# Four chunks of an attention and two-MLP kernel: values placed right behind scores

## The chip, the cores and the metric

One core of a Trainium2 chip runs the whole program. The metric is the device time of one execution in microseconds; lower is better. Matmuls run on TensorE (PE; PEld is its weight load), and the other engines are VectorE (DVE), ScalarE (ACT), GpSimd (POOL) and SyncE (SP), whose queue issues most DMAs.

## The reference, cut to what matters

```python
scores = einsum('bhij,hg->bgij', scale * q @ k.T, w_pre)      # 2 batches, 12 heads, 448 rows, 64 wide
attn = exp(scores - max(scores)); attn = attn / sum(attn)
attn = einsum('bhij,hg->bgij', attn, w_post)
x = (attn @ v) laid out as [896, 768]
h = x @ w_in;  y = (h * clip(h + 3, 0, 6) / 6) @ w_out          # MLP 1, 2048 wide
h = y @ w2_in; out = (P(h) / Q(h)) @ w2_out                     # MLP 2, a rational activation
```

Heads are mixed before and after the softmax (w_pre, w_post), so the twelve heads of a row are needed together.

## The kernel before, in words

The query rows are cut into eight chunks: chunks 0 to 3 of batch 0 and 4 to 7 of batch 1. Six of them have 120 rows, and chunks 3 and 7 have 88. A chunk is worked off in groups of ten rows, twelve groups in a long chunk and nine in a short one. Ten rows times twelve heads fill 120 partitions, and one group is one step of the loop `for s in range(G)`.

In a step for group m, TensorE does the head mix before the softmax, "premix" (lines 306 to 308: three products of one 448-column bank, from the split halves `sh` and `sl` that GpSimd made three groups ahead, lines 294 and 296). VectorE takes the row maximum (line 310), ScalarE the exponential with its sum (line 312). VectorE turns the sum into a reciprocal (lines 320 and 321, `norm`), and ScalarE scales the second mixing matrix with it (line 325, `weigh`, the tile `wr`). Two steps later (`LAG`) TensorE uses it in the "postmix" (line 341: four products, eight instructions, into a bank with the tag A). At the top of the step after that the bank is emptied into `at` by ScalarE (line 348) or, in groups listed in `BYV`, by VectorE (line 346).

Between these steps lie visits of other work. A visit of scores is two calls of `scores` for the next chunk (line 271: twelve products of 64 rows, for four heads). Its banks (tag sc) are copied to `stg` by ScalarE and VectorE in turn (line 274) and spread by DMA into `full`, the layout by row groups (line 252). A visit of values is two calls of `av_unit` for the chunk before (line 363: 32 products with 64 columns, four heads). Its sums `X` are split into a rounded part by ScalarE (line 379) and a remainder by VectorE (line 380). Each `av_unit` also issues on SP the load of values four head pairs ahead (`load_v`, line 136).

In a chunk of twelve steps the scores come in steps 1, 3 and 5 (`SST`) and the values in steps 7, 9 and 11 (`AVST`). So a step with a visit, called heavy here, is always followed by a light one. The queries of the chunk after next are split in steps 9 to 11 (`q_prep` put down for steps 8 and 9; lines 244 on ScalarE and 245 on VectorE). At the end of chunk 2 the keys of batch 1 are split too (lines 236 and 237). From the end of chunk 6 on, pieces of the MLP weights are converted (lines 435 to 460), and ScalarE copies finished rows (line 513).

Every engine works in the order in which the code issues its instructions (`manual_schedule`). `posts`, `xposts`, `aposts`, `preps` and `lows` are lists of work that a step hands to the next one. `full_step` says whether the next step issues `norm` and `weigh` of the group before at its top, ahead of its own maximum, or behind it.

```python
LAG = 2
ONES, BYV = [1, 3, 5], (5, 7, 9)
SST = {12: [1, 1, 3, 3, 5, 5], 9: [0, 0, 2, 2, 4, 4]}
QST = {12: [8, 9], 9: [6, 7]}
AVST = {12: [7, 7, 9, 9, 11, 11], 9: [5, 5, 7, 7, 8, 8]}
AVLAST = [2, 2, 4, 4, 6, 6]
```

Of the kernel before, what the change touches and what calls it, by code (L numbers as in the profile page):

```python
# [7 lines left out]
F32 = mybir.dt.float32  # L8
# [11 lines left out]
B, H, S, D = 2, 12, 448, 64  # L20
JP, JC = 112, 4
GR = 10
GP = GR * H
CH = 120
NCH = 4
MG = CH // GR
NP = H // 2
# [21 lines left out]
def fused_kernel(  # L49
# [23 lines left out]
    chunks, parts = plan()  # L73
# [44 lines left out]
    vraw = {}  # L118
# [211 lines left out]
    def postmix(m):  # L330
# [13 lines left out]
        o = at[C][:, :, :, c0 : c0 + rr]  # L344
        if m in BYV:
            aposts.append(lambda: nc.vector.tensor_copy(out=o, in_=av))
        else:
            aposts.append(lambda: nc.scalar.activation(out=o, in_=av, func=AF.Copy))  # L348

    xps = {}  # L350

    def av_unit(C, h):
        b, r0, n, G = chunks[C]
        if h % 2 == 0:
            return
        if h % 4 == 1:
            tag = "sc" if C + 1 < len(chunks) or h == 1 else "A"
            xps[C] = ps.tile([128, 512], F32, tag=tag, bufs=BUFS[tag], name=f"X{C}_{h}")
        X = xps[C][:, : 2 * CH].rearrange("p (h n) -> p h n", n=CH)
        for jc in range(JC):  # L360
            for hh in (h - 1, h):
                vs = vraw[(C, hh // 2)][:, hh % 2, :].rearrange("p (c d) -> p c d", d=D)
                nc.tensor.matmul(  # L363
                    X[hh % 2 * D : hh % 2 * D + D, hh % 4 // 2, :n], lhsT=vs[:, jc, :], rhs=at[C][:, jc, hh, :n],
                    start=(jc == 0), stop=(jc == JC - 1),
                )
        load_v(*((C, h // 2 + 4) if h // 2 + 4 < NP else (C + 1, h // 2 + 4 - NP)))
        if h % 4 == 3:
            av_evac(C, h, X)

    def av_evac(C, h, X):
        b, r0, n, G = chunks[C]
        c0 = (h - 3) // 2
        t0 = b * S + r0
        src = X[:, :, :n]
        cs, ts_ = slice(c0, c0 + 2), slice(t0, t0 + n)
        o = (x1 if t0 < XRAW else XH)[:, cs, ts_]
        xposts.append([
            lambda: nc.scalar.activation(out=o, in_=src, func=AF.Copy),
            lambda: nc.vector.tensor_tensor(out=XL[:, cs, ts_], in0=src, in1=o.bitcast(F32), op=ALU.subtract),  # L380
        ])
# [190 lines left out]
    LAG = 2  # L572
    ONES, BYV = [1, 3, 5], (5, 7, 9)


    SST = {12: [1, 1, 3, 3, 5, 5], 9: [0, 0, 2, 2, 4, 4]}
    QST = {12: [8, 9], 9: [6, 7]}
    AVST = {12: [7, 7, 9, 9, 11, 11], 9: [5, 5, 7, 7, 8, 8]}
    VAT = 11
    AVLAST = [2, 2, 4, 4, 6, 6]  # L580
# [4 lines left out]
    m = 0  # L585
    for C, (b, r0, n, G) in enumerate(chunks):
# [3 lines left out]
        def add(units, steps):  # L590
            for i, u in enumerate(units):
                sched.setdefault(steps[i * len(steps) // len(units)], []).append(u)

        sst = SST[G] if C else ONES
        if nxt is not None:
# [9 lines left out]
        if C > 0:  # L605
            add([lambda h=h: av_unit(C - 1, h) for h in range(1, H, 2)], [("av", a) for a in (AVST[G] if nxt is not None else AVLAST)])

        for s in range(G):
# [11 lines left out]
            if full_step:  # L620
                norm(m - 1)
                weigh(m - 1)
            for p in posts[:1] + xposts:
                p[0]()
            gsplit(m + 3)()
            if C:
# [13 lines left out]
            for p in posts[1:]:  # L640
                p[1]()
            full_step = bool(s in sst if nxt is not None else s >= 7) or ("av", s) in sched
            for p in xposts + lows:
# [10 lines left out]
            if m >= LAG:  # L654
                postmix(m - LAG)
            for u in sched.get(("av", s), []):
                u()
            for u in sched.get(s, []):
                u()
# [42 lines left out]
    pieces(2)  # L702
    for h in range(1, H, 2):
        av_unit(C, h)
        flush()
# [293 lines left out]
```

## Time and profile before

| what | value |
|---|---|
| median of three runs | 700.87 us (699.5 to 701.43) |
| the profiled execution, its own time | 697.88 us |
| its span, first to last instruction | 696.1 us |
| PE busy | 686.3 us (99%) |
| DVE busy | 532.7 us (77%) |
| ACT busy | 433.8 us (62%) |
| POOL busy | 168.2 us (24%) |
| granted clock of TensorE, mean | 1.000 |

The attention part takes the first 232 us of the span, and the two MLPs the rest. A line of the timeline begins with the start in us from the beginning of the span and the duration; in square brackets stands how long the engine was idle before it and what ended that. A "busy" PE is not one at its peak, because matmuls overlap in a pipeline; what a stage costs is read from the start of one group of products to the start of the next.

### The profile page before, as it was taken

The numbers are of one execution on the slowest core, as the hardware profiler recorded it, in microseconds if no ns is written. First come the engines' busy times: TensorE is split into PE (matmuls) and PEld (weight loads), VectorE is DVE, ScalarE is ACT, GpSimd is POOL, SyncE is SP. The second block draws the span as 40 slices with busy tenths as digits, with TensorE's granted clock in tenths as the row PEclk, the third lists the DMA queues.
The fourth block names the chain that finished last, engine by engine and source line by source line (L and its number), as shares of the span: only waits on it lengthen the run. The fifth ranks groups of instructions, "written<-read, shape, count | busy, mean of one in ns | idle before, by whom it ended". The sixth has DMA issues, their size and how long they took to land.

```text
span 696.1 us, 12343 instructions
## 1 busy us (share of the span) xinstructions
PE 686.3 (99%) x4460; PEld 616.2 (89%) x4461; DVE 532.7 (77%) x964; ACT 433.8 (62%) x881; POOL 168.2 (24%) x195
## 2 busy tenths in 40 slices
PE   8999999999999999999999999999999999999998
PEld 4779888888889888989889888898999999999997
DVE  6855685666657699999976556549999899989991
ACT  6767787787887455555543222237766667669851
POOL 2987775877776200000000000000000000000000
PEclk9999999999999999999999999999999999999999
DMA  5646486545394377675743332517666574755522
GB/s 200 232 133 175 138 215 197 163 139 165 120 265 124 113 246 213 199 218 183 230 156 121 121 122 88 184 54 273 212 240 211 180 267 166 243 181 207 190 81 90
DMA packets 76032, 122.81 MB, mean 176 GB/s; under 512 B 6804, under 2 KB 56260, under 8 KB 75972
## 3 DMA queue, kind: packets, MB, share of 16 engines
q1 hardware_dynamic: 75684, 121.66, 54.2%
q8 instruction: 35, 0.57, 0.3%
q10 hardware_dynamic: 288, 0.37, 0.1%
q14 instruction: 25, 0.20, 0.1%
HBM read 83.39 MB, written 19.27 MB: 147 GB/s over the span
## 4 chain that ended last, share of the span: by engine, by line
PE 93%; DMA 2%; DVE 2%; issue 1%; ACT 1%; POOL 0%; SPq 0%; POOLq 0%; DVEq 0%
PE h L389 11%; PE h L388 11%; PE h L387 11%; PE A L341 9%; PE acc L387 6%; PE acc L389 6%; PE acc L388 6%; PE y L388 6%; PE y L387 6%; PE y L389 6%; PE X L363 5%; PE sc L271 4%; PE M L306 3%; PE M L308 2%; PE M L307 2%; DMA vraw<-in_v_dram 1%
## 5 line engine op out<-in xcount | busy, mean ns | idle before, releaser
L389 PE MATMUL h<-xh,wl 128*128 128x512 f32 (+1 forms) x384 | 139.7, 364 | 0.0
L388 PE MATMUL h<-xl,wh 128*128 128x512 f32 (+1 forms) x384 | 139.5, 363 | 0.0
L387 PE MATMUL h<-xh,wh 128*128 128x512 f32 (+1 forms) x384 | 139.5, 363 | 0.0
L296 POOL TENSOR_TENSOR sl<-full,sh 120x448 fp32r<-120x448 f32 x87 | 100.0, 1149 | 7.3
L341 PEld LDWEIGHTS A<-wr,e 120*112 120x112 f32 x720 | 86.4, 176 | 8.0 <-ACT wr L325 4.0
L310 DVE TENSOR_REDUCE st<-M 120x1 f32<-120x448 f32 x90 | 56.0, 622 | 48.2 <-PE M L308 48.1
L341 PE MATMUL A<-wr,e 120*112 120x120 f32 x720 | 88.9, 266 | 2.2 <-ACT wr L325 2.2
L312 ACT ACTIVATE e<-M,st 120x448 f32<-120x448 f32 x90 | 57.1, 635 | 40.5 <-DVE st L310 34.4
L462 ACT ACTIVATE wh<-wf 128x768 fp32r<-128x768 f32 (+1 forms) x52 | 42.6, 819 | 62.0 <-PE y L388 46.6
L387 PEld LDWEIGHTS h<-xh,wh 128*128 128x128 f32 x384 | 72.1, 188 | 7.5
L388 PEld LDWEIGHTS h<-xl,wh 128*128 128x128 f32 x384 | 72.1, 188 | 7.6
L389 PEld LDWEIGHTS h<-xh,wl 128*128 128x128 f32 x384 | 72.1, 188 | 7.6
L435 ACT ACTIVATE wf<-wraw 128x768 f32<-128x768 f32 (+1 forms) x56 | 49.5, 883 | 42.9 <-DVE wl L463 40.8
L463 DVE TENSOR_TENSOR wl<-wf,wh 128x768 fp32r<-128x768 f32 (+1 forms) x52 | 49.6, 954 | 32.4 <-ACT wh L462 32.4
L388 PE MATMUL y<-gl,wh 128*128 128x384 f32 x192 | 70.1, 365 | 0.0
L387 PE MATMUL y<-gh,wh 128*128 128x384 f32 x192 | 69.9, 364 | 0.0
L389 PE MATMUL y<-gh,wl 128*128 128x384 f32 x192 | 69.5, 362 | 0.0
L294 POOL TENSOR_SCALAR sh<-full 120x448 fp32r<-120x448 f32 x87 | 54.0, 620 | 43.5 <-PE M L307 20.6
L443 DVE SCALAR_TENSOR_TENSOR wf<-wraw,icst,wf 128x768 int32<-128x768 int32 (+1 forms) x56 | 56.5, 1011 | 0.7
L439 DVE SCALAR_TENSOR_TENSOR wf<-wraw,icst,wf 128x768 int32<-128x768 int32 (+1 forms) x56 | 55.9, 999 | 0.9
L348 ACT ACTIVATE at<-A 112x480 f32<-112x480 f32 x87 | 50.3, 579 | 1.8 <-PE A L341 1.8
L389 PE MATMUL acc<-ws,xl 128*128 128x384 f32 x128 | 42.8, 334 | 0.0
(115 smaller groups left out, 1416.3 us busy)
## 6 DMA issues: line engine op xcount, KB each, us to landing
wraw<-in_moe_w_out_dram SPq DMA_DIRECT2D x28, 768.0 KB
wraw<-in_moe_w_in_dram SPq DMA_DIRECT2D x22, 768.0 KB
full<-stg SPq DMA_DIRECT2D x60, 210.0 KB
vraw<-in_v_dram SPq DMA_DIRECT2D x42, 224.0 KB
wpre<-in_moe_w_in_dram SPq DMA_DIRECT2D x10, 768.0 KB
w2h<-wh SPq DMA_DIRECT2D x16, 384.0 KB
w2l<-wl SPq DMA_DIRECT2D x16, 384.0 KB
ws<-w2h SPq DMA_DIRECT2D x16, 384.0 KB
```

Of the source, the lines that this page charges most:

```text
L294: eng.tensor_scalar(out=sh[:r], in0=s[:r], scalar1=1.0, scalar2=0.0, op0=ALU.mult, op1=ALU.add)
L296: return lambda: eng.tensor_tensor(out=sl[:r], in0=s[:r], in1=sh[:r].bitcast(F32), op=ALU.subtract)
L310: nc.vector.tensor_reduce(out=st[:r, 0:1], in_=mt[:r, :S], op=ALU.max, axis=AX.X, negate=True)
L312: nc.scalar.activation(out=e[:r], in_=mt[:r, :S], func=AF.Exp, bias=st[:r, 0:1], accum_out=st[:r, 1:2])
L341: nc.tensor.matmul(av[:, jc], lhsT=e[:r, jc * JP : (jc + 1) * JP], rhs=wr[:r, :, :rr], start=True, stop=True)
L348: aposts.append(lambda: nc.scalar.activation(out=o, in_=av, func=AF.Copy))
L387: nc.tensor.matmul(o, lhsT=wh, rhs=mh, start=first, stop=False)
L388: nc.tensor.matmul(o, lhsT=wh, rhs=ml, start=False, stop=False)
L389: nc.tensor.matmul(o, lhsT=wl, rhs=mh, start=False, stop=last)
L439: nc.vector.scalar_tensor_tensor(out=wi, in0=hw, scalar=icst[:, 0:1], in1=wi, op0=ALU.bitwise_and, op1=ALU.bitwise_or)
L443: nc.vector.scalar_tensor_tensor(out=wi, in0=lw, scalar=icst[:, 1:2], in1=wi, op0=ALU.logical_shift_right, op1=ALU.bitwise_or)
L463: nc.vector.tensor_tensor(out=lv, in0=w, in1=hv.bitcast(F32), op=ALU.subtract)
```

## The change

For chunks 2, 4, 5 and 6 (`joint`: long, not the first two and not the last) the visits are placed anew. Scores come in steps 1, 3 and 6, values in steps 3, 6 and 9. In steps 3 and 6 the values stand right behind the scores, since the scores of a step are now issued before its values. The sums of the values go into a bank with the tag A (that of the postmixes) in these chunks, and into one with the tag sc in the others. In every step of such a chunk `norm` and `weigh` of the group before come at the top. Behind them, ahead of the step's own maximum, come all copies of the scores and both halves of the split of `X`. The postmixes of groups 2, 5, 8 and 9 of these chunks are emptied by VectorE, in steps 5, 8, 11 and step 0 of the next chunk. `av_unit` counts head pairs instead of heads, which changes no instruction.

```diff
--- before.py
+++ after.py
@@ -342,38 +342,35 @@
                 av[:, jc], lhsT=e[:r, jc * JP : (jc + 1) * JP], rhs=wr[:r, :, :rr], start=True, stop=True
             )
         o = at[C][:, :, :, c0 : c0 + rr]
-        if m in BYV:
+        if g in BYV.get(C, ()):
             aposts.append(lambda: nc.vector.tensor_copy(out=o, in_=av))
         else:
             aposts.append(lambda: nc.scalar.activation(out=o, in_=av, func=AF.Copy))
 
     xps = {}
 
-    def av_unit(C, h):
+    def av_unit(C, hp, wide, tag):
         b, r0, n, G = chunks[C]
-        if h % 2 == 0:
-            return
-        if h % 4 == 1:
-            tag = "sc" if C + 1 < len(chunks) or h == 1 else "A"
-            xps[C] = ps.tile([128, 512], F32, tag=tag, bufs=BUFS[tag], name=f"X{C}_{h}")
-        X = xps[C][:, : 2 * CH].rearrange("p (h n) -> p h n", n=CH)
+        i = hp % wide
+        if i == 0:
+            xps[C] = ps.tile([128, 512], F32, tag=tag, bufs=BUFS[tag], name=f"X{C}_{hp}")
+        X = xps[C][:, : wide * CH].rearrange("p (h n) -> p h n", n=CH)
+        vs = vraw[(C, hp)].rearrange("p h (c d) -> p h c d", d=D)
         for jc in range(JC):
-            for hh in (h - 1, h):
-                vs = vraw[(C, hh // 2)][:, hh % 2, :].rearrange("p (c d) -> p c d", d=D)
+            for k in range(2):
                 nc.tensor.matmul(
-                    X[hh % 2 * D : hh % 2 * D + D, hh % 4 // 2, :n], lhsT=vs[:, jc, :], rhs=at[C][:, jc, hh, :n],
+                    X[k * D : k * D + D, i, :n], lhsT=vs[:, k, jc, :], rhs=at[C][:, jc, 2 * hp + k, :n],
                     start=(jc == 0), stop=(jc == JC - 1),
                 )
-        load_v(*((C, h // 2 + 4) if h // 2 + 4 < NP else (C + 1, h // 2 + 4 - NP)))
-        if h % 4 == 3:
-            av_evac(C, h, X)
-
-    def av_evac(C, h, X):
+        load_v(*((C, hp + 4) if hp + 4 < NP else (C + 1, hp + 4 - NP)))
+        if i == wide - 1:
+            av_evac(C, hp - i, hp + 1, X)
+
+    def av_evac(C, p0, p1, X):
         b, r0, n, G = chunks[C]
-        c0 = (h - 3) // 2
         t0 = b * S + r0
         src = X[:, :, :n]
-        cs, ts_ = slice(c0, c0 + 2), slice(t0, t0 + n)
+        cs, ts_ = slice(p0, p1), slice(t0, t0 + n)
         o = (x1 if t0 < XRAW else XH)[:, cs, ts_]
         xposts.append([
             lambda: nc.scalar.activation(out=o, in_=src, func=AF.Copy),
@@ -570,12 +567,14 @@
             aposts.pop(0)()
 
     LAG = 2
-    ONES, BYV = [1, 3, 5], (5, 7, 9)
+    ONES = [1, 3, 5]
+    BYV = {0: (5, 7, 9), **{C: (2, 5, 8, 9) for C in (2, 4, 5, 6)}}
 
 
     SST = {12: [1, 1, 3, 3, 5, 5], 9: [0, 0, 2, 2, 4, 4]}
     QST = {12: [8, 9], 9: [6, 7]}
     AVST = {12: [7, 7, 9, 9, 11, 11], 9: [5, 5, 7, 7, 8, 8]}
+    SSTJ, AVSTJ = [1, 1, 3, 3, 6, 6], [3, 3, 6, 6, 9, 9]
     VAT = 11
     AVLAST = [2, 2, 4, 4, 6, 6]
     full_step = False
@@ -591,7 +590,8 @@
             for i, u in enumerate(units):
                 sched.setdefault(steps[i * len(steps) // len(units)], []).append(u)
 
-        sst = SST[G] if C else ONES
+        joint = C > 1 and nxt is not None and G * GR == CH
+        sst = SSTJ if joint else SST[G] if C else ONES
         if nxt is not None:
             kw = {} if C else {"first": nc.vector.tensor_copy}
             add([lambda h=h: scores(nxt, h, **kw) for h in range(0 if C else FIRST, NP)], sst)
@@ -603,7 +603,9 @@
         if C == NCH - 1:
             add([lambda h=h: k_prep(1, h) for h in range(4, NP)], [0, 1])
         if C > 0:
-            add([lambda h=h: av_unit(C - 1, h) for h in range(1, H, 2)], [("av", a) for a in (AVST[G] if nxt is not None else AVLAST)])
+            tag = "A" if joint else "sc"
+            avst = AVSTJ if joint else AVST[G] if nxt is not None else AVLAST
+            add([lambda h=h: av_unit(C - 1, h, 2, tag) for h in range(NP)], [("av", a) for a in avst])
 
         for s in range(G):
             if s == (5 if C == 1 else 0) and C and C + 2 < len(chunks):
@@ -620,8 +622,14 @@
             if full_step:
                 norm(m - 1)
                 weigh(m - 1)
-            for p in posts[:1] + xposts:
+            first = posts if joint else posts[:1]
+            for p in first + xposts:
                 p[0]()
+            if joint:
+                for p in first + xposts:
+                    p[1]()
+                posts.clear()
+                xposts.clear()
             gsplit(m + 3)()
             if C:
                 for p in posts[:1]:
@@ -639,7 +647,7 @@
                 p[0]()
             for p in posts[1:]:
                 p[1]()
-            full_step = bool(s in sst if nxt is not None else s >= 7) or ("av", s) in sched
+            full_step = joint or bool(s in sst if nxt is not None else s >= 7) or ("av", s) in sched
             for p in xposts + lows:
                 p[1]()
             for p in preps:
@@ -653,9 +661,9 @@
                 next(wpieces)
             if m >= LAG:
                 postmix(m - LAG)
+            for u in sched.get(s, []):
+                u()
             for u in sched.get(("av", s), []):
-                u()
-            for u in sched.get(s, []):
                 u()
             if C == PRE and s == LATE - 1:
                 flush()
@@ -700,8 +708,8 @@
     drain()
     load_units(3)
     pieces(2)
-    for h in range(1, H, 2):
-        av_unit(C, h)
+    for h in range(NP):
+        av_unit(C, h, 2, "sc" if h < 2 else "A")
         flush()
     run(h110)
     h101 = ps.tile([128, 512], F32, tag="M", name="h1_0_1")
```

## Rows read from the trace of the kernel before

**Rows 1.** Page, part 1: busy us, share of the span, instructions.

```profile
PE 686.3 (99%) x4460; PEld 616.2 (89%) x4461; DVE 532.7 (77%) x964; ACT 433.8 (62%) x881; POOL 168.2 (24%) x195
```

**Rows 2.** Windows, chunks 2 and 5: us, busy by engine, clock, DMA share, GB/s.

```profile
67.10:94.93 27.83, 27.83 (x266) 24.21 (x265) 16.75 (x45) 21.84 (x60) 21.88 (x26) 1.00 0.63 176
...
145.92:173.81 27.89, 27.89 (x267) 24.70 (x265) 17.09 (x48) 21.28 (x60) 22.18 (x26) 1.00 0.52 154
```

**Rows 3.** Timeline of PE, chunk 5, steps 7 to 9 in part.

```profile
164.84 0.98 PE L341 MATMUL A<-wr,e 120*112 120x120 f32 x8
165.59 0.44 PE L306 MATMUL M<-sh,wp_h 120*120 120x448 f32 x1
...
166.27 0.98 PE L341 MATMUL A<-wr,e 120*112 120x120 f32 x8
167.18 1.86 PE L363 MATMUL X<-at,vraw 112*64 112x120 f32 x32
168.97 0.46 PE L306 MATMUL M<-sh,wp_h 120*120 120x448 f32 x1
```

**Rows 4.** Timeline, VectorE and ScalarE, one group from maximum to weights.

```profile
222.71 0.62 DVE L310 TENSOR_REDUCE st<-M 120x1 f32<-120x448 f32 x1 [1.00 <-PE M L308]
...
223.37 0.64 ACT L312 ACTIVATE e<-M,st 120x448 f32<-120x448 f32 x1 [0.51 <-DVE st L310]
...
224.13 0.15 DVE L320 TENSOR_SCALAR st<-st 120x1 f32<-120x1 f32 x1 [0.32 <-ACT e L312]
...
224.57 0.40 ACT L325 ACTIVATE wr<-wq,st 120x120 f32<-120x120 f32 x1
```

**Rows 5.** Timeline of VectorE, chunk 5: maximum of step 9, then remainders.

```profile
169.88 0.62 DVE L310 TENSOR_REDUCE st<-M 120x1 f32<-120x448 f32 x1 [1.58 <-PE M L308]
170.43 0.40 DVE L380 TENSOR_TENSOR xl<-X,x 128x240 fp32r<-128x240 f32 x1
170.74 1.42 DVE L245 TENSOR_TENSOR ql<-qraw,qr 128x270 fp32r<-128x270 f32 x1
```

**Rows 6.** Timeline of VectorE, chunk 0, where GpSimd stood idle.

```profile
34.75 0.52 DVE L245 TENSOR_TENSOR ql<-qraw,qr 128x360 fp32r<-128x360 f32 x1
```

**Rows 7.** Line 245 in chunks 4 and 5: count, ns min/median/max.

```profile
L245 DVE TENSOR_TENSOR ql<-qraw,qr x4: 833/1278/1418, 143.2 to 172.9; 128x360 fp32r<-128x360 f32 x2, 128x270 fp32r<-128x270 f32 x2
```

**Rows 8.** Timeline of GpSimd, the same stretch.

```profile
170.71 1.15 POOL L296 TENSOR_TENSOR sl<-full,sh 120x448 fp32r<-120x448 f32 x1
```

**Rows 9.** Line 346, postmix emptied by VectorE: count, ns min/median/max.

```profile
L346 DVE COPY at<-A x3: 656/656/658, 29.8 to 36.8; 112x480 f32<-112x480 f32 x3
```

**Rows 10.** Timeline of PE, chunk 0: four light steps in a row.

```profile
28.14 0.44 PE L306 MATMUL M<-sh,wp_h 120*120 120x448 f32 x1
...
30.80 1.07 PE L341 MATMUL A<-wr,e 120*112 120x120 f32 x8 [0.38 <-ACT wr L325]
...
35.14 0.44 PE L306 MATMUL M<-sh,wp_h 120*120 120x448 f32 x1
```

**Rows 11.** Timeline, end of chunk 2 and start of chunk 3.

```profile
90.08 0.47 PE L306 MATMUL M<-sh,wp_h 120*120 120x448 f32 x1
...
97.05 1.45 DVE L237 TENSOR_TENSOR xh<-kraw,xh 128x448 fp32r<-128x448 f32 x2
...
98.01 0.18 PEld L271 LDWEIGHTS sc<-xh,qr 64*120 64x120 f32 x2 [0.48 <-DVE xh L237]
98.41 0.46 PE L306 MATMUL M<-sh,wp_h 120*120 120x448 f32 x1
```

**Rows 12.** Timeline of PE, chunk 7, step 2.

```profile
206.27 1.07 PE L341 MATMUL A<-wr,e 120*112 120x120 f32 x8 [0.94 <-ACT wr L325]
```

**Rows 13.** Page, part 5: postmix emptied by ScalarE.

```profile
L348 ACT ACTIVATE at<-A 112x480 f32<-112x480 f32 x87 | 50.3, 579 | 1.8 <-PE A L341 1.8
```

**Rows 14.** Timeline of SP's queue, chunk 5: the last spreads.

```profile
162.03 1.61 SPq L252 DMA_DIRECT2D full<-stg  x2
```

**Rows 15.** Timeline of GpSimd, chunk 5, step 9: first split of chunk 6.

```profile
168.31 0.56 POOL L294 TENSOR_SCALAR sh<-full 120x448 fp32r<-120x448 f32 x1 [1.62 <-DMA vraw<-in_v_dram]
```

## The prediction

> **What bounds the kernel now.** I read the shares of busy time first: TensorE is busy for 99% of the span [rows 1]. Then the windows chunk by chunk: chunks 2 and 5 take 27.83 and 27.89 us and TensorE is busy in all of it, at full clock [rows 2]. Last the timeline. From one postmix to the next premix pass 0.75 us (164.84 to 165.59), from that premix to its postmix 0.68, so a light step costs 1.43 us of TensorE. A postmix with values behind it takes 0.91 (166.27 to 167.18), and the values 1.79 to the next premix [rows 3]. So TensorE is nowhere late in these chunks: light and heavy steps alternate, and each heavy one lets the others catch up. The change has no wait to remove there. All it can win is the entry into a visit, and it must not make TensorE wait.
>
> **Fewer visits.** The products stay the same in number and size. Behind a postmix the values start 0.91 - 0.75 = 0.16 us later than a premix would [rows 3]. Each of four chunks gives up two such entries, eight in all. From scores straight to values does not occur in the trace. If it costs as much as an entry, the gain is nothing; if it costs nothing and saves what leaving the scores costs as well (taken as a second 0.16), the gain is 8 x 0.32 = 2.6 us. I take one entry each: -1.3 us. The Trainium skill ("TensorEngine Tiling (Array Packing)", Key Properties) says that a change of tiling mode drains TensorE. Scores use 64 rows and values 64 columns, so by that rule the junction is a drain too and the gain stays at 8 x 0.16 or below, not at 2.6; the 0.16 above agrees that a change of mode costs something.
>
> **What it does to the order.** Heavy steps were 1, 3, 5, 7, 9 and 11; now they are 1, 3, 6 and 9. Light steps now stand in runs: 4 and 5, 7 and 8, and 10, 11 and 0, with step 1's own postmix behind them. In a run a step has 1.43 us. The chain of a group is longer: from the maximum to the exponential 0.66 us, from there to the reciprocal 0.76, from there to the weights 0.44 and 0.40 for them, 0.84 in all [rows 4]. With weights first the reciprocal stands at the head of VectorE's queue and waits for the exponential; the next maximum is queued behind it. That loop is 0.66 + 0.76 + 0.3 (the two small operations, part of the 0.44) = 1.7 us per step, 0.3 more than TensorE needs. Steps 4, 5, 7 and 8 come in pairs behind two visits, and the chain starts ahead of these; so I take 0 for them, at most one step's 0.3 for each of the eight pairs, 2.4.
>
> **The end of chunks 4 and 5.** Here the split of queries falls into steps 10 and 11, which were light and heavy and are now both light. Count from the premix of step 10. Its maximum starts 0.91 later (168.97 to 169.88) and VectorE is free 0.55 after that, at 1.45 [rows 3, 5]. Then comes a query remainder. It takes 0.52 while GpSimd is idle [rows 6], and 0.83 to 1.42 in these two chunks [rows 7], where a split of GpSimd runs beside it (170.71 to 171.86, with the remainder ending at 172.16) [rows 5, 8]. With 1.2 it ends at 2.65. Next is the postmix of group 8, new on VectorE, at 0.66 [rows 9]: 3.31. Only then comes the reciprocal of group 10, and its weights are there 0.84 later, at 4.15. TensorE wanted them at 2 x 1.43 + 0.68 = 3.54, so it waits 0.6. Then 0.3, the maximum of step 11 (0.55), a second remainder (1.2) and the postmix of group 9 (0.66) bring VectorE to 6.02 and the weights of group 11 to 6.86, wanted at 4.97 + 0.6 = 5.57: 1.3 more. Together 1.9 us. With remainders of 0.52 the same sum gives 0.5, with 1.42 it gives 2.3. Chunk 0 has four light steps in a row, with postmixes on VectorE: 28.14 to 35.14 is 7.00 us in place of 5.72, or 1.3 lost, and the wait is for the weights [rows 10]. I take that 1.3 for each chunk, 2.6 for both. The Trainium skill ("SBUF — State Buffer", Who interferes with whom) has VectorE and GpSimd share a port pair, and an operation of VectorE with two inputs there blocks against a reading GpSimd. The remainder that ended 0.30 after GpSimd's split fits that; since GpSimd splits nearly without pause in a light run, the rule would favour 1.9 over 1.3, 1.2 us more for both chunks.
>
> **The end of chunk 2.** From the premix of step 10 to that of chunk 3's step 1 are 8.33 us, and the scores wait for a key remainder on VectorE [rows 11]. In that time lies a values visit of 0.16 + 1.79 = 1.95 that now goes to an earlier place, where TensorE is the bound. If the rest stayed as it is, 6.4 would be left. VectorE's queue, though, holds up to the second key remainder three maxima (1.65), two query remainders (2.4), two postmixes (1.3), two reciprocals (0.6) and two key remainders (1.45 for a pair): 7.4, from 0.91 on, so to 8.3. The second scores follow and the premix 0.4 after (98.01 to 98.41). So 8.7 in place of 6.4: +2.3. With query remainders of 0.52 it is +0.9, with 1.42 +2.7.
>
> **The end of chunk 6.** Weight pieces and row copies load ScalarE and VectorE there, and TensorE already waits 0.94 for weights in step 2 of chunk 7 [rows 12]. A visit of 1.95 that covered this goes; two postmixes go from ScalarE to VectorE and give it 2 x 0.58 back [rows 13]: +0.8. At the least 0, at the most 1.95.
>
> **Queues.** The two loads of values now stand on SP ahead of the four spreads of that visit, and wait until the values are multiplied. The last two spreads take 1.61 us to issue and end at 163.64 [rows 14]; GpSimd's first split of the next chunk started 4.67 later, at 168.31 [rows 15]. Now four spreads (3.2) follow the values of step 6, and perhaps the two loads at up to 0.8 each; with the 4.67 that is 7.9 to 9.5 after the values. The split needs 1.7 more (0.56 and 1.15) [rows 8, 15], so 9.6 to 11.2. Step 0's premix wants its low half 2 x 1.43 + 3.4 + 2 x 1.43 + 0.45 (two of its products) = 9.6 after them. So it comes 0 to 1.6 late, in the stretch that VectorE already holds back by 0.6. I add nothing, up to 1.0 for each of four chunks. Loads of values come sooner than needed, which costs nothing. The bank of the sums is wanted two postmixes later, and its copies come at the top of the next step: 0.
>
> **Sum.** -1.3 + 0 + 2.6 + 2.3 + 0.8 = +4.4 us. The profiled execution took 697.88, its span and 1.8 around it that the change leaves alone; so 702.3. It was 3.0 under the median of the three runs; against 700.87 the forecast is 705.3 us. All low ends give -2.6 + 0 + 1.0 + 0.9 + 0 = -0.7, so 700.2; all high ends 0 + 2.4 + 4.6 + 2.7 + 2.0 + 4.0 = +15.7.
>
> **Rivals.**
> Faster: the ends cost nothing, since VectorE meets GpSimd idle and the weights of groups 10 and 11 arrive in time; the junction saves both costs. For it speaks that late spreads leave GpSimd idle just when the first remainder runs, which then takes 0.52. Against it, the second remainder still finds GpSimd splitting, and chunk 0 lost 1.3 in such a run. Place: the postmixes of groups 10 and 11; it decides when their weights come within 3.54 and 4.97 us of step 10's premix. Price: -2.6, so 698.3.
> No change: the ends cost their low values (0.5, 0.5, 0.9 and 0) and the entries give 1.3 back: +0.6, so 701.5.
> Spreads: the first split of the next chunk comes late, and each later one takes 1.7 against steps of 1.43. At the middle of the bound that is 0.5 in each of four places beyond what VectorE costs: +6.4, so 707.3. For it speaks that GpSimd waited 1.62 there already [rows 15]; against it, that this wait cost TensorE nothing.
>
> **How the numbers follow.** My forecast 0.44, the spreads 0.13, no change 0.25, faster 0.18. A measurement of this kernel tells about 0.3%, 2.1 us, from nothing. Slower by more than that are the first two: 0.57. Within it is the third: 0.25; faster the fourth: 0.18. For 8 times in 10 the range reaches from 698.9, just above the faster rival, to 708.3, the spreads with a little of the high ends. If the forecast's mechanism is the right one, 703 to 708.
>
> **What would show it.** Right: in chunks 4 and 5 no wait of TensorE until step 10, then two, at the postmixes of groups 10 and 11, for weights on ScalarE with VectorE's postmix or query remainder just ahead of the reciprocal; chunk 5 about 1 us above its 27.89; scores to values starting about 0.16 late. Wrong: no waits at chunk ends (then faster or no change), waits for GpSimd's halves in step 0 (the spreads), or waits in steps 4, 5, 7 and 8, where I put nothing.

## The result and the profile after

The changed kernel took 703.99 us (median of 7 runs, 703.65 to 707.75) against 700.43 (7 runs, 697.55 to 701.43) on the same chip: ratio 1.0063, 95% interval 1.0044 to 1.0082. It is slower, by 3.6 us between the medians and by 4.4 by the ratio. The forecast was 705.3, with 0.57 for slower. The profiled execution of the changed kernel has a span of 702.3, 6.2 more than before.

Part 1 of the page after, to set beside [rows 1]: busy us, share of the span, instructions.

```profile
PE 687.2 (98%) x4461; PEld 614.9 (88%) x4461; DVE 539.7 (77%) x980; ACT 433.6 (62%) x865; POOL 169.2 (24%) x195
```

TensorE's busy time hardly grew (686.3 to 687.2), so over 5 of the 6.2 are waits. Six rows of the view of waits, whose columns are us in total, times and longest. Before:

```profile
DVE st L310 <- PE M L308: 48.1, 66, 2.0
...
DVE st L320 <- ACT e L312: 19.4, 34, 0.8
...
PEld A L341 <- ACT wr L325: 4.0, 5, 1.3
...
PEld M L308 <- POOL sl L296: 1.4, 2, 0.9
...
PEld sc L271 <- DVE xh L237: 0.7, 2, 0.5
...
DVE xl L380 <- ACT x L379: 0.5, 2, 0.3
```

After:

```profile
DVE st L320 <- ACT e L312: 32.2, 46, 0.8
...
DVE st L310 <- PE M L308: 18.1, 23, 2.6
...
DVE xl L377 <- ACT x L376: 13.8, 14, 1.5
...
PEld A L341 <- ACT wr L325: 5.7, 8, 1.5
...
PEld M L308 <- POOL sl L296: 3.9, 6, 0.9
...
PEld sc L271 <- DVE xh L237: 3.2, 3, 2.2
```

The rows of VectorE have to be read together. Its maximum waited 48.1 us for TensorE's premix before and 18.1 after; but its reciprocal now waits 32.2 for ScalarE's exponential (19.4 before), and its half of the split of `X` 13.8 for ScalarE's (0.5 before). The three add up to 68.0 before and 64.1 after, and VectorE's idle time is 163.4 us of the span before and 162.6 after. So the fall of the first row shows the new order of VectorE's work, and it is no measure of what was lost. The rows of PEld are TensorE's own waits: for weights (ScalarE, behind VectorE's reciprocal), for GpSimd's low halves and for VectorE's key remainders. All three grew.

To place the time I listed the starts of all 90 premixes in both traces and took the differences. "C5 step 0" is from that premix to the next.

| place | before | after | change | forecast |
|---|---|---|---|---|
| a step of scores and one of values, against a merged and a light step (chunks 2, 5) | 6.37 and 6.39 | 6.20 and 6.22 | -0.17, eight times -1.4 | -1.3 |
| light steps 4, 5, 7, 8 | 1.45 | 1.42 to 1.46 | 0 | 0 |
| C2 step 10 to C3 step 1, less the visit of 1.95 | 6.38 | 9.05 | +2.7 | +2.3 |
| C3 step 3 | 1.45 | 1.85 | +0.4 | 0 |
| C4 step 10 to C5 step 2, less the visit of 1.5 | 7.35 | 9.17 | +1.8 | +1.3 |
| C5 step 10 to C6 step 2, less the visit | 7.33 | 7.67 | +0.3 | +1.3 |
| C6 step 10 to C7 step 3, less the visit | 10.38 | 11.29 | +0.9 | +0.8 |
| sum | | | +4.7 | +4.4 |

From chunk 2's first premix to the end of the span are 628.98 us before and 633.74 after, +4.76, so the table holds nearly all of it. The other 1.4 lie ahead of chunk 2, where both kernels issue the same work: 0.8 ahead of the first premix and 0.6 at the end of chunk 0 (more on that below).

**The merge.** Timeline of TensorE, chunk 5, the end of step 1 (scores alone) and step 3 (scores, then values):

```profile
154.56 0.46 PE L271 MATMUL sc<-xh,qr 64*120 64x448 f32 x2
...
155.96 0.46 PE L306 MATMUL M<-sh,wp_h 120*120 120x448 f32 x1
...
159.01 0.47 PE L271 MATMUL sc<-xh,qr 64*120 64x448 f32 x2
...
160.42 1.86 PE L361 MATMUL X<-at,vraw 112*64 112x120 f32 x32
162.21 0.46 PE L306 MATMUL M<-sh,wp_h 120*120 120x448 f32 x1
```

Scores to premix are 1.40, scores to values 1.41. The junction costs what leaving the scores costs anyway, so one entry is saved and not two.

**The end of chunk 2.** Timeline of VectorE and TensorE in part, with one of GpSimd's splits:

```profile
93.14 0.46 PE L306 MATMUL M<-sh,wp_h 120*120 120x448 f32 x1
...
94.78 0.91 DVE L245 TENSOR_TENSOR ql<-qraw,qr 128x360 fp32r<-128x360 f32 x1
...
96.95 0.66 DVE L245 TENSOR_TENSOR ql<-qraw,qr 128x360 fp32r<-128x360 f32 x1
...
97.31 1.30 POOL L296 TENSOR_TENSOR sl<-full,sh 120x448 fp32r<-120x448 f32 x1
...
97.53 1.56 DVE L237 TENSOR_TENSOR xh<-kraw,xh 128x448 fp32r<-128x448 f32 x1
...
99.02 0.53 DVE L183 TENSOR_SCALAR pa<-pa 128x4 f32<-128x4 f32 x1
...
99.15 0.67 PE L271 MATMUL sc<-xh,qr 64*120 64x448 f32 x4 [0.41 <-DVE xh L237]
...
100.79 2.44 DVE L237 TENSOR_TENSOR xh<-kraw,xh 128x448 fp32r<-128x448 f32 x2
...
101.79 0.47 PE L271 MATMUL sc<-xh,qr 64*120 64x448 f32 x2 [1.77 <-DVE xh L237]
...
102.19 0.47 PE L306 MATMUL M<-sh,wp_h 120*120 120x448 f32 x1
```

VectorE works without a gap through remainders, postmixes, reciprocals and maxima, and TensorE's scores stand behind the key remainders (0.41 and 1.77). The line at 100.79 merges two of them, of 0.95 and 1.57; the second scores wait for the first of these two. [Rows 11] had one wait of 0.48 on its weight load for the same cause.

**The end of chunk 4.** Timeline of VectorE, GpSimd and TensorE in part:

```profile
148.74 0.53 DVE L245 TENSOR_TENSOR ql<-qraw,qr 128x360 fp32r<-128x360 f32 x1
...
149.45 0.57 POOL L294 TENSOR_SCALAR sh<-full 120x448 fp32r<-120x448 f32 x1 [4.18 <-DMA vraw<-in_v_dram]
...
150.07 0.18 PEld L306 LDWEIGHTS M<-sh,wp_h 120*120 120x120 f32 x1 [0.26 <-POOL sh L294]
...
150.53 1.10 DVE L245 TENSOR_TENSOR ql<-qraw,qr 128x360 fp32r<-128x360 f32 x1
...
151.30 0.47 PE L308 MATMUL M<-sl,wp_h 120*120 120x448 f32 x1 [0.56 <-POOL sl L296]
...
153.34 0.47 PE L308 MATMUL M<-sl,wp_h 120*120 120x448 f32 x1 [0.35 <-POOL sl L296]
```

No postmix of groups 10 and 11 waits for weights. What is late is GpSimd's first split of chunk 5, which had waited 4.18 for transfers and starts 5.63 us after the premix of step 9 (143.82). At the end of chunk 5 the first split starts at 177.36, 4.60 after that premix, and TensorE loses only 0.3, in step 1 of chunk 6, where it waits for the second low half; both remainders are short:

```profile
177.36 0.57 POOL L294 TENSOR_SCALAR sh<-full 120x448 fp32r<-120x448 f32 x1 [3.16 <-DMA full<-stg]
...
177.80 0.43 DVE L245 TENSOR_TENSOR ql<-qraw,qr 128x270 fp32r<-128x270 f32 x1
...
179.50 0.55 DVE L245 TENSOR_TENSOR ql<-qraw,qr 128x270 fp32r<-128x270 f32 x1
```

**The end of chunk 6.** Chunk 7, steps 1 and 2: VectorE's weight pieces stand ahead of the reciprocal, and the postmixes wait for weights (0.49 and 1.13; [rows 12] has 0.94).

```profile
209.29 1.43 DVE L434 TENSOR_SCALAR wf<-wf 128x768 int32<-128x768 int32 x1 [0.48 <-ACT wf L432]
...
209.60 1.07 PE L341 MATMUL A<-wr,e 120*112 120x120 f32 x8 [0.49 <-ACT wr L325]
...
212.42 1.07 PE L341 MATMUL A<-wr,e 120*112 120x120 f32 x8 [1.13 <-ACT wr L325]
```

### The profile page after: what moved, and what is told of

The parts are those of the page before. It is cut to its first block, busy times and chain, and to the rows that moved or that the text cites. A ratio compares the mean times of both kernels' runs of the same rounds, so it can differ in the third digit from the quotient of the medians.

```text
span 702.3 us, 12294 instructions
## 1 busy us (share of the span) xinstructions
PE 687.2 (98%) x4461; PEld 614.9 (88%) x4461; DVE 539.7 (77%) x980; ACT 433.6 (62%) x865; POOL 169.2 (24%) x195
## 4 chain that ended last, share of the span: by engine, by line
PE 89%; DVE 4%; DMA 3%; ACT 1%; issue 1%; POOL 1%; SPq 0%; POOLq 0%; ACTq 0%; DVEq 0%
PE h L385 11%; PE h L386 11%; PE h L384 11%; PE A L341 8%; PE acc L384 6%; PE acc L385 6%; PE acc L386 6%; PE y L385 6%; PE y L384 6%; PE y L386 5%; PE X L361 5%; PE sc L271 4%; PE M L306 3%; PE M L308 2%; PE M L307 2%
## 5 line engine op out<-in xcount | busy, mean ns | idle before, releaser
L296 POOL TENSOR_TENSOR sl<-full,sh 120x448 fp32r<-120x448 f32 x87 | 101.7, 1169 | 7.3
L310 DVE TENSOR_REDUCE st<-M 120x1 f32<-120x448 f32 x90 | 55.4, 616 | 18.5 <-PE M L308 18.1
L384 PE MATMUL acc<-ws,xh 128*128 128x384 f32 x128 | 42.8, 334 | 0.0
```

The lines of the kernel that those rows point to most:

```text
L296: return lambda: eng.tensor_tensor(out=sl[:r], in0=s[:r], in1=sh[:r].bitcast(F32), op=ALU.subtract)
L310: nc.vector.tensor_reduce(out=st[:r, 0:1], in_=mt[:r, :S], op=ALU.max, axis=AX.X, negate=True)
L384: nc.tensor.matmul(o, lhsT=wh, rhs=mh, start=first, stop=False)
```

## The experiments

Twelve runs were made as experiments. Eleven are in this table, the changed kernel once more and ten variants of it, with ratios against the kernel before on the same chip; the twelfth is the kernel before itself, profiled again.

| kernel | median us | ratio, 95% interval |
|---|---|---|
| e0_again (the changed kernel) | 705.55 | 1.0084, 1.0063 to 1.0104 |
| e1_loads_behind | 706.66 | 1.0110, 1.0084 to 1.0136 |
| e2_v25 | 706.91 | 1.0102, 1.0075 to 1.0129 |
| e3_x_at_11 | 703.39 | 1.0055, 1.0039 to 1.0070 |
| e8_x11_v25 | 703.26 | 1.0040, 1.0022 to 1.0059 |
| e5_q_early | 703.30 | 1.0046, 1.0025 to 1.0066 |
| e4_not_c2 | 704.67 | 1.0047, 1.0022 to 1.0071 |
| e9_two_chunks | 702.28 | 1.0033, 1.0017 to 1.0049 |
| e11_one_merge | 701.60 | 1.0027, 1.0011 to 1.0043 |
| e6_weights_late | 710.38 | 1.0145, 1.0122 to 1.0167 |
| e12_x11_free | 704.40 | 1.0057, 1.0035 to 1.0079 |

**The changed kernel once more (e0_again).**

> The changed kernel once more, beside the others of this set. Both theories expect 703 to 705 us and about 3.5 to 5 us over the kernel before. Of interest is which ends of chunks repeat: chunk 2's end cost 3.1 us in the first trace (scores wait for key remainders on VectorE), chunk 4's 1.8 (premixes wait for GpSimd's halves), chunk 5's 0.4, chunk 6's 1.0 (postmix waits for weights). If the wait at chunk 4's end is one of transfers that vary, it will be of another size here.

Its profile has the same losses: C3 step 0 at 5.89, C5 steps 0 and 1 at 2.25 and 3.61, C7 steps 1 and 2 at 2.17 and 4.53; from chunk 2 on +4.7 again. The places are no accident of one execution. The sizes vary: the end of chunk 4 loses 1.5 here and not 1.8, with GpSimd's first split of chunk 5 starting 4.96 us after the premix of step 9, and steps 5 and 8 of chunk 3 lose 0.3 to 0.4 each that they don't lose in the first profile.

**Are late spreads the cause (e1_loads_behind)?** The two loads of values that each `av_unit` visit issues are put on SP behind the visit's spreads.

```diff
-        load_v(*((C, hp + 4) if hp + 4 < NP else (C + 1, hp + 4 - NP)))
+        nextv = (C, hp + 4) if hp + 4 < NP else (C + 1, hp + 4 - NP)
+        if tag == "A" and C + 1 < len(chunks):
+            vlater.append(nextv)
...
+            while vlater:
+                load_v(*vlater.pop(0))
```

> The loads of values are issued behind the spreads of their visit. Theory of the spreads (they stand behind loads that wait for the values): GpSimd's first split of the next chunk starts 1 to 2 us earlier, the 1.8 us at chunk 4's end and the 0.4 at chunk 5's end go, about -2 us against the changed kernel. Theory of VectorE's queue (remainders and postmixes ahead of the reciprocal): nothing changes at chunk 2's end (3.1) or chunk 6's (1.0); the total changes by less than 0.5 us.

GpSimd's first split came up to 0.8 us sooner after step 9's premix (chunk 2: 4.23 in place of 5.0; chunk 6: 3.76 in place of 4.43), yet C3 step 0 was 6.72. At the end of chunk 4 the spreads were issued 0.8 sooner, but the split began 4.92 after that premix, as in e0_again (4.96), and C5 steps 0 and 1 stayed at 2.25 and 3.60. So the two loads ahead of the spreads aren't what makes the end of chunk 4 late. The theory of the spreads had promised 2 us; that of VectorE's queue, no change, came nearer. In chunk 7 ScalarE stood idle for 1.38 us ahead of a weight piece, TensorE waited 1.95 for weights, and then its clock fell, as the last section shows.

**Are the postmixes on VectorE the cause (e2_v25)?** Groups 8 and 9 go back to ScalarE.

```diff
-    BYV = {0: (5, 7, 9), **{C: (2, 5, 8, 9) for C in (2, 4, 5, 6)}}
+    BYV = {0: (5, 7, 9), **{C: (2, 5) for C in (2, 4, 5, 6)}}
```

> Only the postmixes of groups 2 and 5 are left to VectorE; those of 8 and 9, which fall into the light run at a chunk's end, go back to ScalarE. Theory of VectorE's queue: chunk 2's end loses the two 0.66 us postmixes from the queue, 3.1 becomes about 1.8; chunk 6's end, where ScalarE is loaded, loses up to 1 us more; in all -1 to 0 us. Theory of the spreads: no change at the ends of chunks 4 and 5, nothing in the total.

C5 steps 0 and 1 fell from 2.27 and 3.62 to 1.85 and 3.25, but C3 step 0 stayed at 5.91 and chunk 7 took 0.4 more. From chunk 2 on the profile loses 5.1, so the copies only change engine. Neither theory held at the places. With two copies less in its queue VectorE began the second key remainder of chunk 2's end 0.55 us sooner after C3's first premix than in e0_again, but that took 1.51 in place of 0.94. And at the end of chunk 4 GpSimd's first split began sooner. In e0_again:

```profile
148.38 0.89 POOL L294 TENSOR_SCALAR sh<-full 120x448 fp32r<-120x448 f32 x1 [3.52 <-DMA vraw<-in_v_dram]
```

In e2:

```profile
149.39 0.56 POOL L294 TENSOR_SCALAR sh<-full 120x448 fp32r<-120x448 f32 x1 [2.99 <-DMA full<-stg]
```

These are 4.96 and 4.43 us after the premix of step 9, although the spreads were issued at the same place (2.36 ahead of it in both). TensorE's weight loads wait 0.30 and 0.36 for the first two low halves there, where in e0_again they wait 0.93 and 0.72.

**Is the missing visit the cause (e3_x_at_11, e8_x11_v25)?** The third values visit goes from step 9 to step 11, in e8 with groups 8 and 9 on ScalarE as well.

```diff
-    SSTJ, AVSTJ = [1, 1, 3, 3, 6, 6], [3, 3, 6, 6, 9, 9]
+    SSTJ, AVSTJ = [1, 1, 3, 3, 6, 6], [3, 3, 6, 6, 11, 11]
```

> The last visit of values moves from step 9 back to step 11, so steps 11 (heavy) and 0 (light) stand again as before the change; the two merged visits stay. Theory that the cover at the chunk's end is what was lost (by whichever engine): all four ends go back to what they were before, -6 us, and only the saved entries are left: -1.3 us against the kernel before, so about -5 us against the changed one. If the run of light steps itself costs (reciprocal at the head of VectorE's queue, 0.3 a step), the now longer run 7 to 10 waits for weights and loses 0.5 to 1 us per chunk, and the kernel ends 1 to 3 us above the one before.

> Values of the joint chunks back in steps 3, 6 and 11 (cover for the end of the chunk), and only the postmixes of groups 2 and 5 on VectorE. Theory (two causes at the ends of the chunks: the missing visit, and the postmixes of groups 8 and 9 in VectorE's queue beside the remainders): with both taken away the ends cost what they did before, the saved entries stay; 698 to 700 us, ratio 0.996 to 1.000 against the kernel before; step 11 of the joint chunks back to about 3.4 us, start of chunk 3 back to 3.5. Rival (the loss sits in late GpSimd splits or in weights-first itself): still 702 or more, ratio 1.004 or more.

Both gained less than half of what was expected: their medians are 0.6 to 2.3 us below those of the changed kernel, where 4 us and more were forecast. In e3 C3 step 0 is still 4.98, and step 11 takes 3.41 to 3.85. In e8 the waits behind the ends are gone (C3 step 0 is 3.02, C5 steps 0 and 1 are 1.45 and 3.04, in place of 6.17 and of 2.27 and 3.62). But step 11 itself takes 3.89 to 4.40 in chunks 4, 5 and 6, against 2.95 to 3.38 for the same work before. Two waits make it up, the same in the next experiment, where they are shown. So the ends do want a visit for cover. The rival's bound (702 or more) was right, and in part for its second reason, weights first.

**Only chunks 4 and 5 (e9_two_chunks),** with the edits of e8.

> Only chunks 4 and 5 changed (where no keys and no weight pieces are split), their values in steps 3, 6 and 11, postmixes of groups 2 and 5 on VectorE. Theory: merges alone, 4 x 0.16 = 0.65 us less than the kernel before, ratio 0.998 to 1.000, and no wait of TensorE at the ends of chunks 4 and 5. Rival (weights at the top of each step hold the maximum behind the reciprocal and cost at the heavy steps by themselves): 0.5 to 1 us more than before, with waits for weights in step 11.

The rival was right on the place, and with 0.5 more in each of chunks 4 and 5 on the price; the whole kernel lost more, in other places. Timeline of VectorE and TensorE, chunk 5, steps 9 to 11:

```profile
173.63 0.16 DVE L321 RECIPROCAL st<-st 120x1 f32<-120x1 f32 x1
...
175.30 0.16 DVE L321 RECIPROCAL st<-st 120x1 f32<-120x1 f32 x1
...
176.19 0.89 PEld L341 LDWEIGHTS A<-wr,e 120*112 120x112 f32 x8 [0.51 <-ACT wr L325]
...
176.96 0.59 ACT L348 ACTIVATE at<-A 112x480 f32<-112x480 f32 x1
...
177.60 1.86 PE L361 MATMUL X<-at,vraw 112*64 112x120 f32 x32 [0.33 <-ACT at L348]
```

With weights first the reciprocals come 1.67 us apart, and a light step of TensorE takes 1.43. In a run of four light steps (7, 8, 9 and 10) the lag of 0.24 a step adds up, and at step 11 the weights are 0.5 late. Then the values wait 0.33 for their A bank, which ScalarE empties late for the same reason. Chunk 2, whose visits are as before here, also lost 1.1: since `sched.get(s)` now runs ahead of the values, key loads go out ahead of the values' loads, and step 11 waits for values:

```profile
87.63 1.11 SPq L128 DMA_DIRECT2D kraw<-in_k_dram  x2
88.85 0.85 SPq L136 DMA_DIRECT2D vraw<-in_v_dram  x2
...
96.97 2.01 PE L361 MATMUL X<-at,vraw 112*64 112x120 f32 x32 [0.92 <-DMA vraw<-in_v_dram]
```

The prediction did not see that move. The changed kernel itself escapes it, because its third visit is in step 9.

**The queries earlier (e5_q_early).**

```diff
-            add([... q_prep ...], QST[G] if C else [6, 8])
+            add([... q_prep ...], ([6, 7] if joint else QST[G]) if C else [6, 8])
```

> As the changed kernel, but the query split of the joint chunks is put down for steps 6 and 7, so that its remainders run in steps 7 and 8 to 9, further from the end of the chunk. Theory (the ends are held up by VectorE's queue): start of chunk 3 down from 6.2 to about 4.7 us, the ends of chunks 4 and 5 down by 0.3 to 0.5 each; the time falls by 1.5 to 2.5 us, to 701.5 to 702.5. Rival (GpSimd's first split sets the ends of chunks 4 to 6): only chunk 2 gains, and the light pair 7 and 8 loses up to 0.5 in each chunk; no change within 1 us.

C3 step 0 fell from 6.17 to 3.96 and C5 steps 0 and 1 to 1.43 and 3.10; step 9 rose by 0.3 to 0.4 in chunks 2, 4 and 5. Chunks 2 to 6 together came to +1.4 against before, where the changed kernel has +3.8. So the query remainders do hold up the end of chunk 2, by VectorE's queue. At the end of chunk 4 the theory isn't shown: there GpSimd's first split began 4.51 us after the premix of step 9 (4.96 in e0_again, 5.63 in the first profile), with the spreads issued at the same place, and without a remainder beside it the high halves took 0.57 and 0.58, where e0_again has 0.89 and 0.84. Of the 2.4 the median shows 0.7 against the first runs of the changed kernel and 2.3 against e0_again, which agrees with the gain without proving its size. The profile itself is the slowest of the twelve executions (708.62): chunk 7 took 25.78 in place of 21.25, with a slow clock in it, as in the last section.

**Chunk 2 left as before (e4_not_c2).**

```diff
-        joint = C > 1 and nxt is not None and G * GR == CH
+        joint = C > 2 and nxt is not None and G * GR == CH
```

> Chunk 2 as in the kernel before, chunks 4, 5 and 6 changed. Forecast by the sum over the profiles: the end of chunk 2 cost 3.1 and its merged visits gave 0.33, so 2.8 us less than the changed kernel, about 701 us, ratio 1.000 to 1.003; start of chunk 3 at 3.5 us as before. Rival (what is lost there comes back elsewhere, since chunk 3 catches up, or the time follows the granted clock more than such waits): within 1 us of the changed kernel.

C3 step 0 is 3.48 again. Chunk 2's last step is 3.90 and not 3.39, with the key loads ahead of the values' loads as in e9. Chunks 2 and 3 together are +0.6, where the changed kernel has +2.7: 2.1 gained in the profile of the 2.8 expected. The medians (704.67 against 703.99 and 705.55) don't confirm it; the ratio (1.0047 against 1.0063 and 1.0084) is lower, but the intervals overlap.

**Weights late again (e6_weights_late).**

```diff
-            full_step = joint or bool(...) or ("av", s) in sched
+            full_step = bool(...) or ("av", s) in sched
```

> As the changed kernel, but weights come at the top only behind a visit, as before; in a light step behind a light one they come behind the maximum. If the loop maximum, exponential, reciprocal, next maximum (1.67 us from one reciprocal to the next, against 1.43 for a step of TensorE) is what makes the weights late at the ends, this gains 0.5 to 1 us per joint chunk, 701.5 to 702.5 us. Rival (the weights are then late by themselves in every light step that follows a light one, as in chunk 0, where such a step took 2.07): steps 5 and 8 of the joint chunks rise from 1.42 to 1.6 or more, and the time is 706 or more.

The rival was right on the time, and by more than it said: 710.38. Its place was one step off: steps 5 and 8 stayed at 1.41 to 1.43, and the loss falls on the postmix of the heavy step behind each light pair: step 6 takes 5.41 (4.78 with weights first) and step 9 3.97 (3.39). Chunk 5, step 6:

```profile
168.19 0.38 ACT L325 ACTIVATE wr<-wq,st 120x120 f32<-120x120 f32 x1
...
168.63 1.07 PE L341 MATMUL A<-wr,e 120*112 120x120 f32 x8 [0.39 <-ACT wr L325]
```

About 0.6 each, twice a chunk, in four chunks: 4.9. Weights first is thus what makes light pairs free; it isn't a cost in pairs, only in longer runs.

**Both waits of step 11 taken away (e12_x11_free).** e8 with the sums of step 11 in an sc bank and weights first only up to step 8.

```diff
-            full_step = joint or bool(...) or ("av", s) in sched
+            full_step = (joint and s < 8) or bool(...) or ("av", s) in sched
-... av_unit(C - 1, h, 2, tag) ...
+... av_unit(C - 1, h, 2, tag if h < 4 else "sc") ...
```

> Both visits merged, values in steps 3, 6 and 11, groups 2 and 5 on VectorE; the sums of step 11 in an sc bank, and weights first only up to step 8, from there on as in the kernel before. In the run with values at 11 and A banks, step 11 took 3.9 to 4.4 us against 3.0 to 3.4 before: 0.5 for weights that are late by then, and 0.3 to 0.5 for the bank that ScalarE had not emptied. Theory: both go, step 11 is at 3.0 to 3.6, the time is 699 to 700.5, ratio 0.998 to 1.002. Rival (late first splits of the next chunk): step 11 stays at 3.8 or more, time 702 or more.

Neither. Step 11 came down to 3.28 to 3.71, but step 10 rose from 1.46 to 2.07 in all four chunks, for weights. That is what [rows 10] shows for chunk 0. Where the maximum comes first in a light step behind a light one, the next step pays 0.6; with weights first the step behind four light ones pays 0.5, and the bank 0.33. A run of four light steps costs either way.

**One merge per chunk (e11_one_merge):** scores in steps 1, 3 and 6, values in 3, 9 and 11; group 2 alone on VectorE.

```diff
-    SSTJ, AVSTJ = [1, 1, 3, 3, 6, 6], [3, 3, 6, 6, 9, 9]
+    SSTJ, AVSTJ = [1, 1, 3, 3, 6, 6], [3, 3, 9, 9, 11, 11]
```

> One values visit behind scores per joint chunk instead of two (step 3); the others in steps 9 and 11 in sc banks, group 2 alone on VectorE, weights first in every step as changed. So no run of more than two light steps, and a visit at the end of the chunk as before. Theory (long light runs at the end of a chunk, without a visit, are what costs): the waits at the ends go, 4 x 0.16 = 0.65 us is saved; 698.8 to 700 us, ratio 0.997 to 1.000. Rival (weights first or the bank of the sums costs by itself): 701 or more.

The closest variant, but still slower (1.0011 to 1.0043), and the rival's bound (701 or more) held. There is no long light run, and chunks 2, 4 and 6 are 0.17 to 0.21 shorter than before, one entry each. In C5 steps 0 and 1 (2.05 and 3.34) the low half of the first split is late, which fits scores that end in step 6 and not 5:

```profile
149.18 0.57 POOL L294 TENSOR_SCALAR sh<-full 120x448 fp32r<-120x448 f32 x1 [4.79 <-PE A L341]
...
149.84 1.45 POOL L296 TENSOR_TENSOR sl<-full,sh 120x448 fp32r<-120x448 f32 x1
...
151.34 0.46 PE L308 MATMUL M<-sl,wp_h 120*120 120x448 f32 x1 [0.34 <-POOL sl L296]
```

Chunk 3 lost 2.4 as well (steps 0, 3, 5 and 8), 0.6 of which the kernel before shows too when it is profiled again. So long light runs and the missing visit are not the whole of the cost; what delays chunk 3 here was not settled. No variant beats the kernel before.

**The kernel before, profiled again (e10_before_again),** one execution, 698.92 us.

> The kernel before, profiled once more. Every profile of a changed kernel lost 0.6 to 3.2 us more than the profile of before between the last step of chunk 0 and the first steps of chunk 1, where all kernels issue the same work (GpSimd's first split of chunk 1 waits for a transfer). If that differs from execution to execution, this profile has its first premix of chunk 1 anywhere from 2.6 to 5 us after that of chunk 0's last step, and the later chunks as before within 0.3 us each; if the changed kernels cause it, it is 2.65 us again within 0.2.

From chunk 0's last premix to chunk 1's first it has 2.73 us, the first profile 2.65; its later chunks agree with those of the first within 0.1, but for C3's last step (4.37 against 3.73), which varies between executions. All twelve profiles of changed kernels have 3.2 to 5.0. In the traces of the changed kernel and of e9 every engine has the same instructions there as before; GpSimd's first split of chunk 1, which waits for transfers, comes later. So it goes with the changed kernels, 0.6 us in the profile after; why is open. It matters for the variants: their first premix of chunk 2 comes at 68.6 to 72.0 us, against 67.1 and 67.5 before and 67.7 and 68.6 in the changed kernel. So 1.5 to 4.9 us of what their profiles lose lies ahead of the chunks that they change, and their whole times say less of the visits than the places do.

## Why the prediction was right, and where its steps were not

The direction, the size (703.99 against 705.3) and the main reason were right: TensorE was hardly ever late in these chunks before, the merges save one entry each, and the light ends of the chunks cost more than that. That the sum came so near (+4.4 against +4.7 in the table) is in part luck: single ends are off by 1.0 down and by 0.5 up. By its own signs the mechanism at the ends of chunks 4 and 5 is not the one forecast. The two waits for weights, of groups 10 and 11, did not come, and waits for GpSimd's halves in step 0, its sign for the spreads rival, did. By its steps:

- **Fewer visits, -1.3:** right, 0.17 each. The Trainium skill ("TensorEngine Tiling (Array Packing)", Key Properties) was used there to hold the gain at one entry, and 1.40 against 1.41 agrees with it: the values behind scores start no sooner than a premix would. They start no later either, so the 0.16 named as a sign there did not show.
- **Light pairs, 0:** right, and e6 shows by what: weights first. The loop forecast at 1.7 us measured 1.67.
- **The ends of chunks 4 and 5, 1.3 each:** the sum (2.6) was near the 2.1 measured, the step was wrong. At the end of chunk 5 the loss is 0.3: both remainders began while GpSimd was at a high half, ahead of its low half, and took 0.43 and 0.55 where the hand sum had 1.2 (with 0.52 the same sum gave 0.5); that a remainder would be short was the faster rival's argument. At the end of chunk 4 the loss is 1.8, and TensorE waited there for GpSimd's halves, not for weights: the mechanism of the spreads rival, which had 0.13. In the four profiles of kernels with this end as changed (the first, e0_again, e1 and e4) the first split begins 4.92 to 5.63 us after the premix of step 9, and TensorE's weight loads wait 0.93 or 0.94 and 0.72 or 0.73 for the first two low halves; in e2 and e5 it begins at 4.43 and 4.51, and these waits are 0.30 and 0.36, and 0 and 0.22. So this end goes by when the split begins and how long the halves take. What makes the split begin later, with the spreads issued at the same place, stays open; e1 shows that it isn't the loads of values ahead of them.
- **The end of chunk 2, +2.3:** the right place and the right wait, with terms that were off against each other. The query remainders took 0.91 and 0.66, not 2.4; the two key remainders ahead of the scores took 1.56 and 0.95, not 1.45 for the pair, and the operation of line 183 (0.53) was not in the sum. [Rows 11] had the key remainders where GpSimd paused for most of the time, and in the light end it splits beside them. The rule of shared ports (the Trainium skill, "SBUF — State Buffer", Who interferes with whom) was applied to the queries and should have been applied to the keys too: the median of such a remainder in the trace after is 0.63, the longest 1.57. The 0.4 in C3 step 3, a wait for weights, was not forecast.
- **The end of chunk 6, +0.8:** right, 0.9, with the weight pieces ahead of the reciprocal.
- **Queues, 0:** the loads of values ahead of spreads cost nothing that e1 could give back. Overlooked was that issuing the units of a step ahead of its values also reorders the key loads (e4, e9).

## What to carry to other kernels

Where the engine that bounds is hardly ever late, putting its visits together can only win what leaving out an entry saves, here 0.17 us apiece; ask first which waits of that engine the heavy steps had hidden. A long wait of another engine is no measure of what it has in hand: VectorE's wait for TensorE fell from 48 to 18 us while its idle time stayed the same. Compare the chain's own period (1.67 us) with a light step (1.43): pairs of light steps are free, longer runs and a light end with extra work are not. When a list of work is issued earlier, follow every kind of unit in it, loads too.

## What the runs showed of the hardware

A wait of TensorE can be followed by a slow clock. In e1, behind a wait of 1.95 us in chunk 7, comes a stretch at half clock. Windows of that stretch: us, busy by engine, clock, DMA share, GB/s.

```profile
205.30:213.10 7.80, 5.89 (x52) 5.10 (x48) 4.50 (x13) 5.28 (x14) 6.39 (x8) 1.00 0.93 250
213.10:215.60 2.50, 2.02 (x11) 1.37 (x11) 2.47 (x5) 2.50 (x8) 2.42 (x4) 0.74 1.08 221
215.60:221.00 5.40, 5.33 (x41) 4.80 (x41) 3.35 (x7) 3.49 (x9) 2.26 (x2) 0.50 0.77 213
```

And TensorE's timeline in it:

```profile
213.14 1.07 PE L341 MATMUL A<-wr,e 120*112 120x120 f32 x8 [1.95 <-ACT wr L325]
...
217.54 3.47 PE L361 MATMUL X<-at,vraw 112*64 112x120 f32 x32
```

At 0.50, which is 1.2 GHz, the values took 3.47 in place of 1.86. The runs of one kernel differ by this: of e0_again, the run with a mean granted clock of 1.000 took 703.13 us and that with 0.992 took 708.57; of the kernel before on the same chip, runs at 1.000 took 698.2 to 699.9 and the one at 0.995 took 702.57. Over these runs the mean clock is 0.9985 before, and 0.996 over all runs of the changed kernel. At a clock of 1.000 the two are 3 to 5 us apart (one run of the changed kernel, three before), about the sum in the table; if all of the time went with the clock, the 0.3% between the means would be an estimated 2 us of 700. The profiles of e5 and e12 fall in the same place (0.64 from 217 to 222, and 0.78 from 220 to 224). The profile after doesn't: behind its wait of 1.13 the clock stays at 1.00. So when a wait ends in such a stretch was not settled.
